# Threshold attention and a tanh-shrink MLP on one core: the shared tiles of two head pairs made one duo, turns and transfers re-timed

## The chip, the cores and the metric

One core of a Trainium2 chip runs the whole kernel. The metric is the device time of one execution in microseconds, and the median of several runs is compared. The profiler records one execution, and all views of the profile are of that one.

## The reference

Two layers follow each other. The first is attention with a threshold, for 8 batches, 8 heads, 576 rows and 64 columns:

```python
scores = scale * np.matmul(q, k.transpose(0, 1, 3, 2))
thresh = np.max(scores, axis=-1, keepdims=True) - tau
scores = np.where(scores >= thresh, scores, -1000000000.0)
scores = scores - np.max(scores, axis=-1, keepdims=True)
attn = np.exp(scores)
attn = attn / (np.sum(attn, axis=-1, keepdims=True) + 1e-09)
return np.matmul(attn, v).astype(np.float32)
```

The second takes the heads side by side as rows `x` of 512 (4608 rows), and computes `h = x @ w_in` (512 to 2048), `g = h - tanh(h)` and `g @ w_out` (2048 to 512). All inputs and the output are float32.

## The kernel before

**Pairs, tiles, duos.** The work goes by pairs of heads: 32 pairs, four to a batch (a batch is called a block below). A head has 576 rows, that is four tiles of 128 rows and a rest of 64. The rests of both heads of a pair fill one *shared* tile, so a pair has nine tiles (`TPP = 9`) and the kernel 288. Tile number `i` is tile `j = i % 9` of pair `p = i // 9`: 0 to 3 are head 0, 4 is the shared one, 5 to 8 are head 1. Two neighbouring tiles of one head form a *duo* ("A" and "B", `kind`), which shares one maximum buffer, one `nb`, one transpose and one `pT`. The shared tile ("M") goes alone: it has an `nb` of its own, buffers `zm` padded to 640 columns, and a transpose of five blocks where a duo has one of nine.

**A tile's way.** `scores` multiplies a tile of qT with kT and with kS (kT with its halves exchanged, which adds the low-order parts of the float16 split) into PSUM, and VectorE scales it into `sc` and takes its maximum (L337). `shift` makes `nb`, the threshold (L354). `kink` is a steep Prelu on ScalarE (L374), which gives `z`. For pairs 0 to 5 (`on_pe`) TensorE transposes z (L394). From pair 6 on the DMA crossbar does (`zT<-z`, L382, issued from SP). `weights` is the exponential on ScalarE (L403 or L411), which gives `pT`. `attend` multiplies pT with v (L440, for the shared tile L429) into `psO`; v has a column of ones that collects the sum. The five blocks of a tile's weights are four of 128 keys and one of 64; in a duo, the two blocks of 64 lie in one block, in rows 0 to 63 and 64 to 127, and v's buffer `vb` has two matching chunks (4 and 5), each zero in the other half. `norm` divides a head's output by its sum on VectorE (L454, L455, and L460 for the shared tile, at head 0). `emit_x` transposes a pair's output on TensorE (L472, L478) and copies it (L485, L486) into the MLP's input.

**Preparing a pair.** `load` brings k, q, v from SP. `split` (GpSimd, L190 to L194) makes the float16 parts khl and qhl. `turn` transposes them: nine matmuls on TensorE (L241) into the same two-buffer PSUM ring `big` that the scores use, then a copy on VectorE (L264). For k, GpSimd then makes kS with two copies (L270). From pair 8 on, q of the odd pairs and of pair 30 is turned by the crossbar instead (`q_by_dma`, L253). `split_v` (GpSimd, L222 to L227) fills vb.

**MLP.** Beside the attention of a block, the MLP of the block before it runs: `hidden` (L495), tanh on ScalarE (L508), `g` on VectorE (L514), `project` (L521), and every fourth step a copy `yo` (L534) and a store (L537), which is issued when the next one is ready. A step is four matmuls of 512 columns. `layers` deals about one step to a slot (fewer in the first block), and none to the first four slots of a block.

**Order.** No planner sets the order: the program is written out slot by slot, `s` from -8 to 292, and every engine takes its instructions in the order in which the slots issue them. In slot `s` come: `shift` of tile s+7, `scores` of tile s+8 (`AHEAD = 8`), `kink` of tile s+5, tanh, `weights` of tile s, an MLP step, g, stores, `attend` of tile s-2 (`LAG = 2`) with `norm` and `emit_x`, then the steps of `plan` for the slot, and casts of the MLP's weights on GpSimd (until about slot 59). (For the first four pairs weights and attend come four slots earlier.) `plan` puts the preparation of pair p a number `d` of slots before its first scores, in slot 9p - 8 - d: loads at d = 16, 15, 14 for k, q, v, splits of k and q at 8 and 7, turn k at 5, split_v at 4, turn q at 3, or at 5 by the crossbar.

**Buffers** that matter here: PSUM ring `big` two (scores and turns), `psO` one, `psH` two, `psY` one; pT three, zT six, z four, raw two of each of k, q, v, vb four.

Of the kernel before, what the change touches and what calls it, by code (L numbers as in the profile page):

```python
# [18 lines left out]
def kernel(  # L19
# [11 lines left out]
    nc = tc.nc  # L31
# [15 lines left out]
    NPAIR = B * HPAIR  # L47
    DM_C = d_model // P
    DF_C = d_ff // P
    TPP = 9  # L50
    NTILE = NPAIR * TPP

# [34 lines left out]
    for i in range(NV):  # L87
# [3 lines left out]
        nc.gpsimd.memset(vb[0:64, :, 4, D : D + 1], 1.0)  # L91
        nc.gpsimd.memset(vb[64:P, :, 5, D : D + 1], 1.0)
        vbs.append(vb)

    NM = 2
    zms = []
    for i in range(NM):
        zm = const.tile([P, 5 * P], BF16, name=f"zm{i}")
        nc.vector.memset(zm[:, S : 5 * P], -STEEP)
        zms.append(zm)  # L100

    mx3 = []
# [39 lines left out]
    def load(p, t):  # L144
        b, h0 = p // HPAIR, 2 * (p % HPAIR)
        hs = slice(h0, h0 + 2)
        src = {"k": k, "q": q, "v": v}[t]
        eng = nc.sync
        r = raws[p, t] = raw_pool.tile([P, 10, D], F32, name=f"{t}raw", tag=t)
        n = 8 if t == "v" else 10  # L150
        eng.dma_start(
            out=r[:, 0:n, :].rearrange("p (h c) d -> p h (c d)", h=2)[:, :, 0 : 4 * D],
            in_=src[b, hs, 0:512, :].rearrange("h (p c) d -> p h (c d)", c=4),
        )
        rem = src[b, hs, 512:S, :].rearrange("h s d -> s h d")
        if t == "v":
            eng.dma_start(out=r[0:64, 8:10, :], in_=rem)
        else:
            eng.dma_start(out=r[:, 4, :], in_=rem)
# [136 lines left out]
    REM = (slice(512, 576), slice(576, 640))  # L296
    scs, mxs, nbs, zs, zts, pts, ops = {}, {}, {}, {}, {}, {}, {}

    def kind(j):

        return "M" if j == 4 else "A" if j in (0, 2, 5, 7) else "B"

    def scores(i):
        p, j = divmod(i, TPP)
        qT, kT, kS = mats[p, "q"], mats[p, "k"], mats[p, "ks"]
        ps = ps_big.tile([P, 1024], F32, name="psS", tag="big")
        main, rem, lo = slice(0, 512), slice(512, 576), 0
        if kind(j) == "B":
            main, rem, lo = slice(512, 1024), slice(448, 512), 448
        if j == 4:  # L310
            qrem = REM
            if q_by_dma(p):
                qrem = (slice(512, 640, 2), slice(513, 640, 2))
            for n, kk in enumerate((kT, kS)):
                for dst, srcs in ((main, MAIN), (rem, REM)):
                    for hh in range(2):
                        nc.tensor.matmul(  # L317
                            out=ps[64 * hh : 64 * hh + 64, dst],
                            lhsT=qT[:, qrem[hh]], rhs=kk[:, srcs[hh]],
                            start=(n == 0), stop=(n == 1),  # L320
                        )
        else:
            hh = int(j > 4)
            lhs = qT[:, j * P : (j + 1) * P]
            for n, kk in enumerate((kT, kS)):
                for dst, src in ((main, MAIN[hh]), (rem, REM[hh])):
                    nc.tensor.matmul(  # L327
                        out=ps[:, dst], lhsT=lhs, rhs=kk[:, src],
                        start=(n == 0), stop=(n == 1),
                    )  # L330
        sc = sc_pool.tile([P, S], F32, name="sc")
        if kind(j) == "B":
            mx = mxs[i] = mxs.pop(i - 1)
        else:
            mx = mxs[i] = mx3[i // 2 % len(mx3)]
        c = int(kind(j) == "B")
        nc.vector.tensor_scalar(  # L337
            out=sc, in0=ps[:, lo : lo + S], scalar1=SC, scalar2=None,
            op0=ALU.mult, op1=ALU.max, accum_out=mx[:, c : c + 1],
        )  # L340
        scs[i] = sc

    def shift(i):

        kd = kind(i % TPP)
        if kd == "A":
            return
        mx = mxs.pop(i)
        nb = st_pool.tile([P, 9], F32, name="nb", tag="nb")
        o, m = nb[:, 0:1], mx[:, 0:1]  # L350
        if kd == "B":
            o = nb.rearrange("p (a b) -> p a b", b=3)[:, :, 0:2]
            m = mx.rearrange("p (a b) -> p a b", b=4)[:, :, 0:3]
        nc.vector.tensor_scalar(  # L354
            out=o, in0=m, scalar1=-1.0, scalar2=tau, op0=ALU.mult, op1=ALU.add
        )
        if kd == "B":
            nbs[i - 1], nbs[i] = nb[:, 0:1], nb[:, 1:2]
        else:
            nbs[i] = nb[:, 0:1]  # L360

    def kink(i):
        sc, nb = scs.pop(i), nbs.pop(i)
        kd = kind(i % TPP)
        if kd == "B":
            zt = zs.pop(i - 1)
            z = zt[:, S:W]
        elif kd == "A":
            zt = zs[i] = z_pool.tile([P, W], BF16, name="z")
            z = zt[:, 0:S]  # L370
        else:
            zt = zms[i // TPP % NM]
            z = zt[:, 0:S]
        nc.scalar.activation(  # L374
            out=z, in_=sc, func=ACT.Prelu, bias=nb, scale=1.0, alpha=STEEP
        )
        if on_pe(i):
            zts[i] = zt
        elif kd != "A":
            n = 5 if kd == "M" else TPP  # L380
            zts[i] = zt_pool.tile([P, TPP, P], BF16, name="zT")
            nc.sync.dma_start_transpose(out=zts[i][:, 0:n, :], in_=zt)  # L382

    def weights(i):


        kd = kind(i % TPP)
        n, off = {"A": (4, 0), "M": (5, 0), "B": (5, 4)}[kd]
        if on_pe(i):
            z = zts.pop(i)  # L390
            pl, tag = (ps_h, "h") if i % 2 and i < HPAIR * TPP else (ps_y, "y")
# [23 lines left out]

    def attend(i):

        p, j = divmod(i, TPP)
        kd, vb = kind(j), vbs[p % NV]
        if kd == "A":  # L420
            return
        if j in (1, 6):
            ops[p, int(j > 4)] = ps_o.tile([P, 6, D + 1], F32, name="psO", tag="o")
        po = ops[p, int(j > 4)]
        if kd == "M":
            pt = pts.pop(i)

            for c in range(5):
                nc.tensor.matmul(  # L429
                    out=po[:, 4:6, :], lhsT=pt[:, c * P : (c + 1) * P],  # L430
                    rhs=vb[:, :, c, :], start=(c == 0), stop=(c == 4),
                )
            return
        pt, hh = pts.pop(i), int(j > 4)

        for ab in range(2):
            blocks = [(4 * ab + ab + c, c) for c in range(4)]
            blocks.append((4, 4 + ab))
            for n, (blk, c) in enumerate(blocks):
                nc.tensor.matmul(  # L440
                    out=po[:, (j - 1 - 5 * hh) + ab, :],
                    lhsT=pt[:, blk * P : (blk + 1) * P], rhs=vb[:, hh, c, :],
                    start=(n == 0), stop=(n == 4),
                )

    osb = {}

    def norm(p, hh):
        po = ops.pop((p, hh))
        if hh == 0:  # L450
            osb[p] = o_pool.tile([P, 5, 2, D], BF16, name="osb")
        n = 5 - hh
        rc = st_pool.tile([P, 5], F32, name="rc", tag="rc")
        nc.vector.reciprocal(out=rc[:, 0:n], in_=po[:, 0:n, D])  # L454
        nc.vector.tensor_tensor(  # L455
            out=osb[p][:, 0:4, hh, :], in0=po[:, 0:4, 0:D],
            in1=rc[:, 0:4].unsqueeze(2).to_broadcast([P, 4, D]), op=ALU.mult,
        )
        if hh == 0:
            nc.vector.scalar_tensor_tensor(  # L460
                out=osb[p][:, 4, :, :], in0=po[:, 4:6, 0:D], scalar=rc[:, 4:5],
                in1=own, op0=ALU.mult, op1=ALU.mult,
            )
# [55 lines left out]
    def project(m, ms, part, ps, last, cols=slice(0, d_model)):  # L519
# [5 lines left out]
        if part == 3:  # L525
# [8 lines left out]
                nc.vector.tensor_copy(out=yo, in_=ps)  # L534
            if m < B:
                rows = out[m * S : m * S + MB, :].rearrange("(p c) n -> c p n", c=4)
                stores.append(lambda: nc.sync.dma_start(out=rows[ms], in_=yo))  # L537
            else:
                for h in range(2):
                    b = 2 * ms + h  # L540
                    eng = nc.scalar if h and nc_ < d_model else nc.sync
                    stores.append(
                        lambda b=b, h=h, eng=eng: eng.dma_start(
                            out=out[b * S + MB : (b + 1) * S, cols],
                            in_=yo[64 * h : 64 * h + 64, :],
                        )
                    )
# [107 lines left out]
    for p in range(1, NPAIR):  # L655
        first = TPP * p - AHEAD
        for d, f in PREP[3 if p == 1 else 0 :]:
            d -= p == 1 and d in (3, 5)
            plan.setdefault(first - d, []).append(lambda p=p, f=f: f(p))
        d = 5 if q_by_dma(p) else 3 - (p == 1)  # L660
        plan.setdefault(first - d, []).append(lambda p=p: turn(p, "q"))

    load(0, "v")
# [27 lines left out]
    for s in range(-AHEAD, NTILE + LAG + 3):  # L691
# [37 lines left out]
        for i in atts.pop(s, []):  # L729
            pp, jj = divmod(i, TPP)  # L730
            if i < NTILE:
                attend(i)
            if i < NTILE and jj in (4, 8):
                norm(pp, int(jj > 4))
            if jj == 1 and pp:
                emit_x(pp - 1)
        for step in plan.pop(s, []):
            step()
# [61 lines left out]
```

## Time and profile before

| | before |
|---|---|
| median of 8 runs | 536.83 us (536.49 to 538.35) |
| the profiled execution | 537.43 us, of which the span of the profile is 535.6 |
| TensorE busy | 513.5 us, 96% |
| VectorE busy | 427.4 us, 80% |
| ScalarE busy | 438.0 us, 82% |
| GpSimd busy | 290.0 us, 54% |
| transposes of z, z with padding, q by the crossbar | 104, 26, 13 |
| loads of v; stores of 256 KB | 32 and 32 (a large and a small one); 32 |
| DMA traffic | 85.76 MB, 160 GB/s in the mean |

The busy times are shares of the whole span, which has stages with different limits, so the table alone does not say which engine sets the time. The time that TensorE's instructions are shown for is modelled at its end and overlaps with the next instruction; how far the starts of two matmuls lie apart is the better measure. "PEld" is the load of a matmul's stationary side. A wait for several signals is put down to the one that came last.

### The profile page before, as it was taken

How to read it: one execution, taken by the hardware profiler on the slowest of the kernel's cores; microseconds unless marked ns; L12 is line 12 of the kernel's file. 1: busy time of each engine (PE TensorE's matmuls, PEld its weight loads, DVE VectorE, ACT ScalarE, POOL GpSimd, SP SyncE). 2: the span in 40 equal slices, each digit the busy share in tenths (PEclk: the TensorE clock that was granted, in tenths of full speed). 3: DMA queues.
4: the chain of work that ended last, by engine and by line, in shares of the span. 5: the costliest groups of instructions: out<-in, count | busy, mean ns of one | idle time of the engine just before them, and what ended most of it. 6: DMA issues, size and time to landing. Idle time of an engine off the chain costs nothing.

```text
span 535.6 us, 13042 instructions
## 1 busy us (share of the span) xinstructions
PE 513.5 (96%) x4782; PEld 288.5 (54%) x4782; DVE 427.4 (80%) x1202; ACT 438.0 (82%) x630; POOL 290.0 (54%) x390
## 2 busy tenths in 40 slices
PE   8989899999999999999999999999999999999997
PEld 4666565555555555555555555555455455444444
DVE  5889878989888988889888988898888888554440
ACT  5999888998898989899888989898989989543330
POOL 7999995767555666666555755565665720000000
PEclk9999999999999999999999999999999999999999
DMA  7554657999899799799999999899988975401113
GB/s 211 174 185 146 207 163 139 198 189 184 174 177 184 178 188 196 168 181 188 187 187 185 192 192 187 157 182 197 189 157 184 188 153 111 105 21 39 39 41 78
DMA packets 204768, 85.76 MB, mean 160 GB/s; under 512 B 172320, under 2 KB 197152, under 8 KB 204704
## 3 DMA queue, kind: packets, MB, share of 16 engines
q1 hardware_dynamic: 204112, 84.51, 74.9%
q8 instruction: 37, 0.61, 0.5%
q10 hardware_dynamic: 592, 0.43, 0.3%
q14 instruction: 27, 0.22, 0.1%
HBM read 36.70 MB, written 9.44 MB: 86 GB/s over the span
## 4 chain that ended last, share of the span: by engine, by line
PE 67%; DVE 14%; POOL 8%; DMA 3%; issue 3%; ACT 2%; SPq 1%; DVEq 0%; POOLq 0%; ACTq 0%
PE psY L521 21%; PE psH L495 17%; PE psS L327 14%; DVE sc L337 6%; PE psO L440 5%; DVE g L514 3%; PE psS L317 3%; PE psHt L495 3%; POOL kS L270 2%; PE ps_k L241 2%; DMA qT<-qhl 2%; DVE kT L264 1%; DVE yo L534 1%; POOL w_in_sb L628 1%; POOL khl L194 1%
## 5 line engine op out<-in xcount | busy, mean ns | idle before, releaser
L337 DVE TENSOR_SCALAR_CACHE_REDUCE sc<-psS 128x576 f32<-128x576 f32 x288 | 216.1, 752 | 23.2 <-PE psS L327 14.7
L374 ACT ACTIVATE z<-sc,nb 128x576 bf16<-128x576 f32 x256 | 193.5, 768 | 19.0 <-DVE nb L354 18.9
L521 PE MATMUL psY<-w_out_sb,g 128*128 128x512 bf16 (+1 forms) x592 | 146.0, 374 | 0.8 <-DVE yo L534 0.8
L411 ACT ACTIVATE pT<-zT 128x1152 f16<-128x1152 bf16 (+1 forms) x130 | 138.9, 1068 | 1.6 <-PE psS L327 1.0
L270 POOL COPY kS<-kT 64x1152 f16<-64x1152 f16 x62 | 70.7, 1141 | 127.5 <-DVE nb L354 125.8
L495 PE MATMUL psH<-xT,w_in_sb 128*128 128x512 bf16 x480 | 124.0, 379 | 2.3 <-DVE g L514 2.3
L327 PE MATMUL psS<-kT,qT 128*128 128x512 f16 (+1 forms) x512 | 104.4, 285 | 7.2 <-DVE sc L337 4.2
L508 ACT ACTIVATE th<-psH 128x512 f32<-128x512 f32 x128 | 75.4, 589 | 36.9 <-PE psH L495 35.7
L327 PEld LDWEIGHTS <-qT 128*128 128x128 f16 x1024 | 72.5, 97 | 57.1 <-issue 9.2
L327 PE MATMUL psS<-kS,qT 128*128 128x512 f16 x496 | 101.4, 286 | 0.8 <-POOL kS L270 0.7
L514 DVE SCALAR_TENSOR_TENSOR g<-th,psH 128x512 bf16<-128x512 f32 x128 | 87.3, 682 | 17.9 <-ACT th L508 17.9
L521 PEld LDWEIGHTS <-g 128*128 128x128 bf16 x592 | 50.7, 98 | 56.8 <-issue 4.0
L495 PEld LDWEIGHTS <-w_in_sb 128*128 128x128 bf16 x576 | 49.2, 98 | 58.2 <-issue 4.5
L440 PEld LDWEIGHTS <-pT 128*128 128x128 f16 x1280 | 55.7, 98 | 25.2 <-issue 1.9
L440 PE MATMUL psO<-vb,pT 128*128 128x65 bf16 x1280 | 61.2, 193 | 0.0
L194 POOL TENSOR_TENSOR khl<-kraw,khl 128x576 f16<-128x576 f32 x31 | 39.7, 1279 | 2.6
L194 POOL TENSOR_TENSOR qhl<-qraw,qhl 128x576 f16<-128x576 f32 x31 | 39.7, 1279 | 2.7
L403 ACT ACTIVATE pT<-psZ 128x640 f16<-128x640 bf16 (+1 forms) x54 | 35.4, 658 | 5.8 <-PE psZ L394 5.4
L264 DVE COPY kT<-ps_k 128x1152 f16<-128x1152 f16 x31 | 23.4, 756 | 14.0 <-PE ps_k L241 14.0
L534 DVE COPY yo<-psY 128x512 f32<-128x512 f32 (+1 forms) x31 | 21.1, 682 | 13.1 <-PE psY L521 11.1
L455 DVE TENSOR_TENSOR osb<-psO,rc 128x256 bf16<-128x256 f32 x64 | 27.2, 424 | 2.2
L354 DVE TENSOR_SCALAR nb<-mx 128x6 f32<-128x6 f32 (+1 forms) x160 | 24.5, 153 | 2.3
(81 smaller groups left out, 509.3 us busy)
## 6 DMA issues: line engine op xcount, KB each, us to landing
vraw<-in_v_dram SPq DMA_DIRECT2D x32, 256.0 KB, 3.5
out_dram<-yo SPq DMA_DIRECT2D x32, 256.0 KB, 3.0
kraw<-in_k_dram SPq DMA_DIRECT2D x31, 256.0 KB, 3.3
qraw<-in_q_dram SPq DMA_DIRECT2D x31, 256.0 KB, 3.7
wt<-in_moe_w_in_dram SPq DMA_DIRECT2D x8, 512.0 KB, 4.3
wt<-in_moe_w_out_dram SPq DMA_DIRECT2D x8, 512.0 KB, 4.4
zT<-z SPq DMA_TRANSPOSE x104, 3.5
kraw<-in_k_dram SPq DMA_DIRECT2D x32, 32.0 KB, 3.0
```

What stands on the lines that cost most here:

```text
L194: nc.gpsimd.tensor_tensor(out=hl[:, :, 1, :], in0=x, in1=hl[:, :, 0, :], op=ALU.subtract)
L270: nc.gpsimd.tensor_copy(out=o, in_=i)
L327: nc.tensor.matmul(out=ps[:, dst], lhsT=lhs, rhs=kk[:, src], start=(n == 0), stop=(n == 1),)
L337: nc.vector.tensor_scalar(out=sc, in0=ps[:, lo : lo + S], scalar1=SC, scalar2=None, op0=ALU.mult, op1=ALU.max, accum_out=mx[:, c : c + 1],)
L374: nc.scalar.activation(out=z, in_=sc, func=ACT.Prelu, bias=nb, scale=1.0, alpha=STEEP)
L403: nc.scalar.activation(out=pt[:, off * P : (off + n) * P], in_=ps[:, 0 : n * P], func=ACT.Exp)
L411: nc.scalar.activation(out=pt[:, 0 : n * P], in_=zts.pop(i)[:, 0:n, :], func=ACT.Exp)
L440: nc.tensor.matmul(out=po[:, (j - 1 - 5 * hh) + ab, :], lhsT=pt[:, blk * P : (blk + 1) * P], rhs=vb[:, hh, c, :], start=(n == 0), stop=(n ...
L495: nc.tensor.matmul(out=ps, lhsT=w_in_sb[:, c, n * P : (n + 1) * P], rhs=xs[m][:, c, :] if m < B else xR[:, c, :, :], start=(c == 0), stop= ...
L508: nc.scalar.activation(out=th, in_=ps, func=ACT.Tanh)
L514: nc.vector.scalar_tensor_tensor(out=gs[m][:, n, :], in0=th, scalar=-1.0, in1=ps, op0=ALU.mult, op1=ALU.add,)
L521: nc.tensor.matmul(out=ps, lhsT=gs[m][:, n, ms * P : (ms + 1) * P], rhs=w_out_sb[:, n, cols], start=(n == 0), stop=(n == DF_C - 1),)
```

## The change

- **Shared duo.** The shared tile moves to the end of an even pair and to the beginning of an odd one, so that the shared tiles of two pairs are neighbours and form a duo like any other. `kind` is now the parity of i, and `place` gives the pair, head and tile of i. The kind "M" and the buffers `zm` go. The transposes become one of nine blocks for every two tiles.
- **Attend.** A duo's block of 64 + 64 keys is multiplied once with both chunks of v (130 columns, for both tiles), then eight matmuls of 65 columns add to that. The shared duo's two halves are done by `attend_shared` when psO of the head with which they share a buffer is there: head 1 of the even pair, head 0 of the odd one. `skip_group_check` is a flag of the builder.
- **Norms.** They follow the tiles: jj = 3 (even pair) or 4 (odd) for head 0, jj = 0 of the next pair (even) or 8 (odd) for head 1. `emit_x` of an even pair comes one slot later.
- **Turns.** Turn k is at d = 6 (odd) or 3 (even) from pair 5 on. Turn q on TensorE is at d = 2, only for pair 3 still at 3.
- **q by the crossbar.** Its turn is at d = 7, and the splits of k and q of these pairs are at 10 and 9.
- **Queues.** The loads of v from pair 8 on, and the stores of blocks 0 to 5, are issued from GpSimd's queue in place of SP's.

```diff
-    def kind(j):
-        return "M" if j == 4 else "A" if j in (0, 2, 5, 7) else "B"
+    def kind(i):
+        return "AB"[i % 2]
+    def place(i):
+        p, j = divmod(i, TPP)
+        j = j - p % 2
+        return (p, None, 4) if j in (-1, 8) else (p, j // 4, j % 4)
...
-        eng = nc.sync
+        eng = nc.gpsimd if t == "v" and p >= 2 * HPAIR else nc.sync
...
     def kink(i):
...
-            n = 5 if kd == "M" else TPP
             zts[i] = zt_pool.tile([P, TPP, P], BF16, name="zT")
-            nc.sync.dma_start_transpose(out=zts[i][:, 0:n, :], in_=zt)
+            nc.sync.dma_start_transpose(out=zts[i], in_=zt)
...
     def attend(i):
...
-        for ab in range(2):
-            blocks = [(4 * ab + ab + c, c) for c in range(4)]
-            blocks.append((4, 4 + ab))
-            for n, (blk, c) in enumerate(blocks):
-                nc.tensor.matmul(
-                    out=po[:, (j - 1 - 5 * hh) + ab, :],
-                    lhsT=pt[:, blk * P : (blk + 1) * P], rhs=vb[:, hh, c, :],
-                    start=(n == 0), stop=(n == 4),
-                )
+        p, hh, t = place(i)
+        vb, pt = vbs[p % NV], pts[i]
+        if hh is None:
+            attend_shared(p - 1, 0, pt)
             return
+        if t == 1:
+            ops[p, hh] = ps_o.tile([P, 6, D + 1], F32, name="psO", tag="o")
+            if p % 2 and hh == 0:
+                attend_shared(p, 1, pts.pop(i - 2))
+        po = ops[p, hh]
+        nc.tensor.matmul(
+            out=po[:, t - 1 : t + 1, :], lhsT=pt[:, 4 * P : 5 * P],
+            rhs=vb[:, hh, 4:6, :], start=True, stop=False, skip_group_check=True,
+        )
+        for n in range(8):
+            ab, c = divmod(n, 4)
+            blk = 5 * ab + c
+            nc.tensor.matmul(
+                out=po[:, t - 1 + ab, :], lhsT=pt[:, blk * P : (blk + 1) * P],
+                rhs=vb[:, hh, c, :], start=False, stop=(n == 7), skip_group_check=True,
+            )
+    def attend_shared(p, ab, pt):
+        vb = vbs[p % NV]
+        for n in range(5):
+            blk, c = ((5 * ab + n, n) if n < 4 else (4, 4 + ab))
+            nc.tensor.matmul(
+                out=ops[p, 1 - p % 2][:, 4:6, :], lhsT=pt[:, blk * P : (blk + 1) * P],
+                rhs=vb[:, :, c, :], start=(n == 0), stop=(n == 4),
+            )
...
-                stores.append(lambda: nc.sync.dma_start(out=rows[ms], in_=yo))
+                eng = nc.gpsimd if m < B - 2 else nc.sync
+                stores.append(lambda: eng.dma_start(out=rows[ms], in_=yo))
...
             d -= p == 1 and d in (3, 5)
+            if d in (7, 8) and q_by_dma(p):
+                d = d + 2
+            if d == 5 and p >= 5:
+                d = 6 if p % 2 else 3
...
-        d = 5 if q_by_dma(p) else 3 - (p == 1)
+        d = 7 if q_by_dma(p) else 3 - (p == 1 or p % 2 == 0 or p >= 5)
...
-            if i < NTILE and jj in (4, 8):
-                norm(pp, int(jj > 4))
-            if jj == 1 and pp:
+                odd = pp % 2
+                if jj == 3 + odd:
+                    norm(pp, 0)
+                elif odd and jj in (0, 8):
+                    norm(pp - (jj == 0), 1)
+            if pp and jj == 1 + pp % 2:
                 emit_x(pp - 1)
```

## The prediction

> **What bounds the kernel now.** I read the page's first part, then the time windows by stage, the list of waits, and the timeline where the windows left a question. From the page (a group's columns: line, engine, operation, tiles, count | busy us, mean ns of one | idle before it):
>
> ```profile
> PE 513.5 (96%) x4782; PEld 288.5 (54%) x4782; DVE 427.4 (80%) x1202; ACT 438.0 (82%) x630; POOL 290.0 (54%) x390
> L440 PE MATMUL psO<-vb,pT 128*128 128x65 bf16 x1280 | 61.2, 193 | 0.0
> L270 POOL COPY kS<-kT 64x1152 f16<-64x1152 f16 x62 | 70.7, 1141 | 127.5 <-DVE nb L354 125.8
> ```
>
> The windows (stretch, its length, busy us and instructions of PE, PEld, DVE, ACT, POOL; then clock, DMA share, GB/s) show that 96% is a mean of stages:
>
> ```profile
> 26.00:37.00 11.00, 10.33 (x149) 7.50 (x149) 10.00 (x31) 10.62 (x19) 10.41 (x14) 1.00 0.52 169
> 100.00:115.00 15.00, 13.87 (x154) 8.21 (x150) 13.96 (x40) 14.86 (x22) 10.87 (x13) 1.00 0.98 178
> 250.00:350.00 100.00, 99.00 (x932) 54.97 (x930) 87.54 (x250) 89.49 (x124) 57.14 (x73) 1.00 0.95 182
> ```
>
> Until about 72 us ScalarE (10.62 of 11.00) and GpSimd (10.41) are full, and TensorE has gaps. Around 100 us ScalarE is full. From about 130 us to the end TensorE is: 99.00 of 100. There only fewer TensorE instructions or fewer TensorE waits shorten the kernel. Its waits from 100 to 440 us:
>
> ```profile
> POOL kS L270 <- DVE nb L354: 121.9, 24, 6.6
> DVE kT L264 <- PE ps_k L241: 10.9, 17, 1.1
> PE psS L327 <- DVE sc L337: 2.2, 11, 0.3
> PEld L327 <- DMA qT<-qhl: 2.6, 3, 1.4
> PE psS L327 <- DMA qT<-qhl: 1.4, 2, 1.0
> ```
>
> The two last lines partly tell of the same moments (weight load and matmul both stand still), so the crossbar's q costs TensorE about 1.4 us, not 4.0. GpSimd's 121.9 us are idle time before kS, which waits for the copy kT.
>
> [...] ten of 65 columns take 257.98 to 258.29 us, 31 ns each; five of 130 take 260.15 to 260.44, 58 ns each (below). [...] No run before issues a load from GpSimd. [...]
>
> **Part 1, attend.** Before, each of 128 duos takes ten matmuls of 65 columns; after, one of 130 and eight of 65. The columns are 650 both times. A pair of 65s costs 62 ns, a 130 costs 58: 4 ns a duo, 128 x 4 = 0.5 us[...]. The 193 ns mean of the group row is latency and must not be used, nor 61.2/1280 = 48 ns. **I take -0.6 (0 to -0.9).** The shared part keeps its 160 matmuls of 130 columns, the shared scores all of theirs.
>
> **Part 2, ten transposes become nine.** In pairs 6 to 31, 26 exponentials of 640 columns at 726 ns (18.9 us) become 13 of 1152 at 1154 (15.0): ScalarE saves 3.9 us, 0.15 a pair. VectorE's nb go from 160 to 144 of 155 ns, 24.5 us to 22.3. SP loses 13 transposes of about 1.3 us issue time. In steady state all this lies beside TensorE's 99% and is worth nothing. In pairs 6 to 8, where ScalarE is full, 3 x 0.15. **-0.4 (0 to -1).** A shared pT lives two slots longer in the ring of three: its next writer comes at slot i+6, its last reader at i+4, so two slots (3.2 us) stay: nothing.
>
> **Part 3, the turns of k and q.** Count slots modulo 18 from the first of an even pair. Norms: before 6, 10, 15, 1; after 5, 11, 15, 1. Turn k: before 5 and 14; after (pair 5 on) 7 and 13. Turn q on TensorE: before 7, after 8. Before, q followed a norm at once; at 89 us this cost 0.82 us:
>
> ```profile
> 89.28 0.67 PE L241 MATMUL ps_q<-ident_f,qhl 128*128 128x128 f16 x9
> 89.36 0.42 DVE L455 TENSOR_TENSOR osb<-psO,rc 128x256 bf16<-128x256 f32 x1
> ...
> 90.77 0.41 PE L327 MATMUL psS<-kT,qT 128*128 128x512 f16 x2 [0.82 <-DVE sc L337]
> ```
>
> The norm (0.19+0.42+0.34 us) held back sc, and the turn had taken the other buffer of the ring of two. All waits of TensorE for sc are 4.2 us on the full list of waits; about 0.25 us in each block stands where the MLP pauses, and stays. **-1.5 (0 to -3)** with the smaller waits from 86 to 131 us. Against it stands **kS**. An even pair's k is now turned three slots ahead of its scores instead of five. The chain in the trace:
>
> ```profile
> 257.98 0.48 PE L440 MATMUL psO<-vb,pT 128*128 128x65 bf16 x10
> 258.29 0.67 PE L241 MATMUL ps_k<-ident_f,khl 128*128 128x128 f16 x9
> ...
> 259.06 0.76 DVE L264 COPY kT<-ps_k 128x1152 f16<-128x1152 f16 x1 [0.44 <-PE ps_k L241]
> ...
> 259.95 2.32 POOL L270 COPY kS<-kT 64x1152 f16<-64x1152 f16 x2 [5.86 <-DVE nb L354]
> ...
> 260.15 0.46 PE L429 MATMUL psO<-vb,pT 128*128 128x130 bf16 x5
> ...
> 260.44 0.41 PE L327 MATMUL psS<-kT,qT 128*128 128x512 f16 x2
> ```
>
> kS ends 262.27 - 258.29 = 3.98 us after the turn starts. TensorE's work until it reads kS: the turn 0.51, slot 8 (scores 0.49, an MLP step 0.86, turn q 0.51) 1.86, slot 9 (0.49 + 0.86 + attend 0.31) 1.66, the kT half of the scores 0.24: 4.27. The margin is 0.29 us, and a norm two slots earlier (0.95 us) may leave VectorE late. GpSimd itself is free by then: split_v is in slot 6, its next split waits in slot 9. **+0.7 (0 to +6.5)**, over 13 even pairs, 0.05 each. Odd pairs have six slots; that their turn k now shares slot 13 with emit_x (0.42 + 0.21 us of VectorE) costs nothing there.
>
> **Part 4, q for the crossbar two slots sooner.** Splits and turn move together, so their distance stays; load to split shrinks from eight slots to six (9.6 us, against 3.3 to land). SP comes late today because transposes wait for ScalarE ahead of q in one queue:
>
> ```profile
> 421.51 1.31 SPq L253 DMA_TRANSPOSE qT<-qhl  x1
> ...
> 425.10 0.42 PE L327 MATMUL psS<-kT,qT 128*128 128x512 f16 x2 [0.95 <-DMA qT<-qhl]
> ```
>
> Two slots (3.2 us) cover 0.95. But the splits for it now follow kS of slot 7 at once: kS until about slot 9.5, two splits of 2.6 us, qhl about slot 12.8, so SP, due at 12, waits about a slot; the z transposes behind it have about two. **-1.4 (0 to -1.6).**
>
> **Part 5, v loads and stores from GpSimd.** 24 pairs x 2 loads and 6 blocks x 4 stores, 72 issues, leave SP (0.54 to 0.65 us each, 42 us) for GpSimd. No row shows one[...]. A store waits for yo, but is issued a step of y (8 slots) later, so splits and kS behind it don't wait; v loads come ten slots ahead of split_v, raw buffers long free. The cover is GpSimd's idle time before kS. **0 (-0.5 to +3).**
>
> **Sum:** -0.6 - 0.4 - 1.5 + 0.7 - 1.4 = -3.2 us on the profiled execution, 537.43 (span 535.6 and 1.8 around it): 534.2. That execution lies 0.6 over the median of 536.83, so I forecast 533.6. Little is to be had beyond: TensorE's own waits from 100 to 440 us add to 6.3 us in that list, and the first 72 us are GpSimd's, where only turn q of pairs 2 and 4 moves, by a slot.
>
> **Rivals.** *A, as above* (0.67): 530.5 to 535.6. *B, a wait for a wait* (0.13): q comes in time, but TensorE stands as long at kS or sc; gains of 3.9 are eaten: 536 to 537.5. For it: VectorE at 88% and ScalarE at 89% have little give. Against: kT waited for TensorE, not TensorE for it. *C, kS late* (0.13): in even pairs kT gets behind one sc and one g (0.75 + 0.68 us). Each such stall is 1.43 - 0.29 = 1.1 us, in all 13 pairs 14.8, and 548 at the end. It decides from 0.3 us a pair (3.9/13), when kT starts 0.6 us later after its turn than now; at 0.5 us it gives 6.5 - 3.9 = +2.6: 539.4. For it: the norm in slot 5. Against: VectorE stood idle 0.44 us before kT. *D, GpSimd as bound* (0.04): three issues fill its 6.2 us a pair from 2.1 us each[...]. *E* (0.03): the crossbar engines are full at 0.95 whoever issues, and SP gains nothing; about 535.0, the sum without part 4.
>
> **Numbers.** Faster 0.69 (A and most of E), same 0.14 (B, the rest of E), slower 0.17 (C, D); 0.2%, 1.1 us, is about what a measurement can tell. The range takes A's lower bounds together at 529.5 and C's nearer half at 540.
>
> **Right if** the waits show no DMA qT, PE waits for kS stay under 1 us in all, windows from 150 us show TensorE at 99% with about 0.1 us less per block of four pairs, and GpSimd's idle time before kS falls to 50 us or more. **Wrong if** kS heads TensorE's waits, or GpSimd's idle time is gone and khl or qhl are waited for.

## The result, and the profile after

| | before | after |
|---|---|---|
| median | 537.25 us (32 runs, 536.41 to 538.57) | 571.5 us (11 runs, 562.89 to 577.2) |
| profiled execution (span) | 537.43 us (535.6) | 569.36 us (567.6) |
| ratio after to before | | 1.0544 [1.0523, 1.0566] |

The change makes the kernel slower by 5.4%, where 533.6 us were forecast. (The ratio leaves out runs over 1.5% above the fastest of a kernel, so it stands for some 566.5 us, and a difference that this text takes from the median of all eleven, 571.5, would be 5.0 us smaller with it.)

First the page of the kernel after: busy times, the granted clock in 40 slices, the two large DMA queues (packets, MB, share of 16 engines' span), and groups (line, engine, operation, tiles, count | busy us, mean ns of one | idle before it and what ended most of it).

```profile
PE 521.8 (92%) x4651; PEld 293.9 (52%) x4651; DVE 424.4 (75%) x1184; ACT 437.1 (77%) x617; POOL 334.8 (59%) x462
...
PEclk9999999988989799897998999999999899999999
...
q1 hardware_dynamic: 188592, 70.71, 63.5%
q0 software_dynamic: 4608, 13.37, 9.4%
...
L400 ACT ACTIVATE pT<-zT 128x1152 f16<-128x1152 bf16 x117 | 135.0, 1154 | 32.7 <-DMA zT<-z 32.6
L265 POOL COPY kS<-kT 64x1152 f16<-64x1152 f16 x62 | 70.7, 1141 | 117.7 <-DVE nb L349 116.1
L428 PE MATMUL psO<-vb,pT 128*128 128x65 bf16 x1024 | 54.4, 196 | 0.0
L421 PE MATMUL psO<-vb,pT 128*128 128x130 bf16 x128 | 28.5, 223 | 25.4 <-ACT pT L400 25.4
```

TensorE's share fell from 96% to 92% with 131 instructions fewer. GpSimd's busy time grew by 44.8 us, which are the new issues, and its idle time before kS only fell from 125.8 to 116.1 us: GpSimd is not what is short. New are two idle times: ScalarE's exponential waits 32.6 us for zT, a crossbar transpose, and TensorE's attend waits 25.4 us for that exponential. The granted clock has slices at 7 and 8, early and in the middle. Queue q0 is GpSimd's own: 13.37 MB in 4608 packets, 2.9 KB each in the mean.

The windows of the same stretches as before, and one short one (stretch, length, busy us and instructions of PE, PEld, DVE, ACT, POOL; clock, DMA share, GB/s):

```profile
26.00:37.00 11.00, 9.75 (x139) 7.16 (x137) 10.15 (x31) 10.39 (x18) 10.41 (x14) 1.00 0.52 171
100.00:115.00 15.00, 14.16 (x143) 8.47 (x140) 14.71 (x41) 14.48 (x21) 9.98 (x14) 1.00 0.86 157
250.00:350.00 100.00, 92.69 (x823) 51.46 (x821) 81.05 (x232) 82.65 (x112) 66.40 (x89) 0.95 0.89 169
350.00:470.00 120.00, 115.81 (x1056) 64.78 (x1054) 102.27 (x290) 105.34 (x143) 83.97 (x114) 0.99 0.91 177
124.00:130.00 6.00, 3.80 (x23) 2.13 (x24) 1.39 (x5) 4.88 (x6) 3.65 (x6) 0.56 0.80 184
```

Up to 115 us nothing is lost. From 250 to 350 us TensorE starts 823 matmuls where it started 932 before (911 in `e1_all_on_sp` below, which has the same instructions), and no other engine is full. From 124 to 130 us the granted clock is 0.56. Counted in the trace, ScalarE has six long waits for zT: they begin between 120 and 292 us, 34 to 35 us apart, one in every two pairs (18 slots), and make up 28.7 of its 32.6 us. A block takes 67 to 68 us there, and about 58 afterwards, as in the kernel before.

The waits of the kernel after from 100 to 470 us (engine, line, what it waited for: us in all, times, longest):

```profile
ACT pT L400 <- DMA zT<-z: 32.6, 10, 6.0
...
PE psO L421 <- ACT pT L400: 25.4, 9, 5.3
```

No wait of TensorE for qT is left, and none for kS over 0.3 us. One of the stalls in its timeline (start us, duration, engine, line, operation; in brackets the idle time before it and what ended it):

```profile
149.01 1.15 ACT L400 ACTIVATE pT<-zT 128x1152 f16<-128x1152 bf16 x1
...
149.69 14.40 SPq L371 DMA_TRANSPOSE zT<-z  x4
...
150.10 0.72 POOL L146 DMA_DIRECT2D vraw<-in_v_dram  x1
...
150.81 0.60 POOL L152 DMA_DIRECT2D vraw<-in_v_dram  x1
...
151.99 1.15 ACT L400 ACTIVATE pT<-zT 128x1152 f16<-128x1152 bf16 x1
...
155.45 0.62 POOL L537 DMA_DIRECT2D out_dram<-yo  x1
...
157.79 1.03 PE L520 MATMUL psY<-w_out_sb,g 128*128 128x512 bf16 x4
...
160.94 1.16 ACT L400 ACTIVATE pT<-zT 128x1152 f16<-128x1152 bf16 x1 [5.98 <-DMA zT<-z]
...
162.15 0.27 PE L421 MATMUL psO<-vb,pT 128*128 128x130 bf16 x1 [3.34 <-ACT pT L400]
```

The exponentials stand at 149.01, 151.99 and then 160.94: for the last, ScalarE stood idle 5.98 us. Before that, a v load leaves GpSimd at 150.10, 0.41 us after SP began to issue transposes of z at 149.69. SP's first three issues from there on take 1.67, 2.51 and 6.38 us where the median is 1.38: SP is held up in issuing. The store of 155.45 falls into the same stretch. Its windows:

```profile
146.00:152.00 6.00, 6.00 (x53) 3.28 (x51) 5.83 (x17) 4.89 (x9) 4.08 (x5) 1.00 1.03 214
152.00:158.00 6.00, 6.00 (x57) 2.98 (x56) 4.32 (x15) 2.95 (x5) 5.51 (x10) 1.00 1.18 86
158.00:162.00 4.00, 0.82 (x4) 0.20 (x2) 1.45 (x3) 1.06 (x1) 3.33 (x6) 1.00 1.29 140
```

The last two columns are to be read together: from 152 to 158 us the DMA engines show as full as ever (1.18), yet only 86 GB/s pass, against 214 just before. (The share adds up the times of all packets, which overlap, so it can exceed 1.) Counted in the trace, the packets of the v load's 288 KB took from 151.9 to 158.5 us, 6.5 us, where 1 to 4 are usual outside the six stalls. Those of 4 KB took 0.65 us each in the mean, where 0.17 is the median of all. Of the 256-byte packets of the transposes most still took 18 ns, but some took up to 1 us, so that their mean from 152 to 158 us was 69 ns, against 26 over the stretch from 100 to 480 us. The view of the tile zT in the kernel after sums it up: duration of an issue, minimum/median/maximum, and from issue to landing:

```profile
L371 SPq DMA_TRANSPOSE zT<-z x117: 1272/1377/6376, 85.4 to 490.1; - x117
...
DMA to landing us min/median/max: 3.2/3.5/11.6
```

In the kernel before, the last line was:

```profile
DMA to landing us min/median/max: 2.5/3.4/6.8
```

The median hardly moved, the tail is new.

### The profile page after: what moved, and what is told of

Read it like the earlier page. It is cut to its first block, busy times and chain, and to the rows that moved or that the text cites. A ratio compares the mean times of both kernels' runs of the same rounds, so it can differ in the third digit from the quotient of the medians.

```text
span 567.6 us, 12777 instructions
## 1 busy us (share of the span) xinstructions
PE 521.8 (92%) x4651; PEld 293.9 (52%) x4651; DVE 424.4 (75%) x1184; ACT 437.1 (77%) x617; POOL 334.8 (59%) x462
## 3 DMA queue, kind: packets, MB, share of 16 engines
q0 software_dynamic: 4608, 13.37, 9.4%
## 4 chain that ended last, share of the span: by engine, by line
PE 60%; POOL 10%; DMA 10%; DVE 7%; ACT 7%; issue 5%; SPq 0%; ACTq 0%; POOLq 0%; DVEq 0%
PE psY L520 18%; PE psH L494 16%; PE psS L327 13%; DMA zT<-z 9%; PE psO L428 3%; ACT z L364 3%; PE psHt L494 2%; POOL kS L265 2%; DVE sc L337 2%; DVE g L513 2%; PE ps_k L236 2%; ACT pT L400 2%; POOL khl L189 1%; ACT th L507 1%; PE psS L318 1%
## 5 line engine op out<-in xcount | busy, mean ns | idle before, releaser
L364 ACT ACTIVATE z<-sc,nb 128x576 bf16<-128x576 f32 x288 | 216.6, 769 | 33.6 <-DVE nb L349 31.6
L400 ACT ACTIVATE pT<-zT 128x1152 f16<-128x1152 bf16 x117 | 135.0, 1154 | 32.7 <-DMA zT<-z 32.6
L265 POOL COPY kS<-kT 64x1152 f16<-64x1152 f16 x62 | 70.7, 1141 | 117.7 <-DVE nb L349 116.1
L494 PE MATMUL psH<-xT,w_in_sb 128*128 128x512 bf16 x480 | 128.6, 392 | 3.5 <-DVE g L513 3.5
L327 PE MATMUL psS<-kT,qT 128*128 128x512 f16 (+1 forms) x512 | 107.0, 291 | 4.0 <-DVE sc L337 2.1
L327 PEld LDWEIGHTS <-qT 128*128 128x128 f16 x1024 | 75.9, 99 | 62.0 <-issue 10.9
L327 PE MATMUL psS<-kS,qT 128*128 128x512 f16 x496 | 103.8, 292 | 0.0
L494 PEld LDWEIGHTS <-w_in_sb 128*128 128x128 bf16 x576 | 50.3, 100 | 61.3 <-issue 11.4
L428 PE MATMUL psO<-vb,pT 128*128 128x65 bf16 x1024 | 54.4, 196 | 0.0
L421 PE MATMUL psO<-vb,pT 128*128 128x130 bf16 x128 | 28.5, 223 | 25.4 <-ACT pT L400 25.4
L428 PEld LDWEIGHTS <-pT 128*128 128x128 f16 x1024 | 45.2, 99 | 9.3
L392 ACT ACTIVATE pT<-psZ 128x512 f16<-128x512 bf16 (+1 forms) x54 | 35.0, 652 | 5.4 <-PE psZ L383 5.2
L421 PEld LDWEIGHTS <-pT 128*128 128x128 f16 x128 | 12.5, 98 | 39.8 <-ACT pT L400 28.7
L533 DVE COPY yo<-psY 128x512 f32<-128x512 f32 (+1 forms) x31 | 21.1, 682 | 14.4 <-PE psY L520 12.7
```

The costliest lines, as they stand in the source:

```text
L265: nc.gpsimd.tensor_copy(out=o, in_=i)
L327: nc.tensor.matmul(out=ps[:, dst], lhsT=lhs, rhs=kk[:, src], start=(n == 0), stop=(n == 1),)
L364: nc.scalar.activation(out=z, in_=sc, func=ACT.Prelu, bias=nb, scale=1.0, alpha=STEEP)
L400: nc.scalar.activation(out=pt[:, 0 : n * P], in_=zts.pop(i)[:, 0:n, :], func=ACT.Exp)
L421: nc.tensor.matmul(out=po[:, t - 1 : t + 1, :], lhsT=pt[:, 4 * P : 5 * P], rhs=vb[:, hh, 4:6, :], start=True, stop=False, skip_group_check ...
L428: nc.tensor.matmul(out=po[:, t - 1 + ab, :], lhsT=pt[:, blk * P : (blk + 1) * P], rhs=vb[:, hh, c, :], start=False, stop=(n == 7), skip_gr ...
```

## The experiments

Theory 1, formed from these lines: the transfers issued from GpSimd hold up the crossbar's transposes in the DMA engines, zT is late, TensorE stands, and its granted clock falls. The rivals: the new order or the sooner q alone makes zT late, whoever issues the loads; a collision of a certain slot, which a shift of the load would remove; or the bytes, not the queue. All times are medians; "ratio" is to the kernel before, run beside it.

**All loads and stores back on SP** (`e1_all_on_sp`), the rest of the change kept:

```diff
-        eng = nc.gpsimd if t == "v" and p >= 2 * HPAIR else nc.sync
+        eng = nc.sync
...
-                eng = nc.gpsimd if m < B - 2 else nc.sync
+                eng = nc.sync
```

> The kernel after, with v loads and stores back on SP's queue; all else of the change stays. Theory 1 (two queues at once: transfers from GpSimd's queue run in the DMA engines between the packets of the crossbar's transposes, zT lands late, ScalarE waits for zT and TensorE for pT): the waits of ScalarE for zT fall from 32.6 us to under 2 us, the granted clock is 1.00 again, and the time is 531 to 537 us. Theory 2 (the new order itself makes the transposes late, since q's transpose and the splits stand in front of them): the waits for zT stay above 20 us and the time stays above 560 us. Theory 3 (kS late on even pairs): TensorE waits for kS for several us and the time is 538 to 548 us.

533.49 us, ratio 0.9925 [0.9905, 0.9946]. This one part is worth 38.0 us (33.0 with the 566.5 us of the ratio) and the sign; the kernel without it beats both. Its page, window and tile zT:

```profile
PE 510.6 (96%) x4651; PEld 289.5 (54%) x4651; DVE 423.9 (80%) x1184; ACT 436.3 (82%) x617; POOL 290.4 (55%) x390
```

```profile
250.00:350.00 100.00, 99.12 (x911) 55.95 (x911) 88.29 (x251) 89.53 (x121) 60.36 (x78) 1.00 0.91 183
```

```profile
L371 SPq DMA_TRANSPOSE zT<-z x117: 1242/1344/2953, 85.4 to 454.1; - x117
...
DMA to landing us min/median/max: 3.2/3.6/6.8
```

TensorE is back at 99.12 of 100 us, and no zT lands later than 6.8 us. The waits from 100 to 440 us, ScalarE's and then TensorE's:

```profile
ACT pT L400 <- DMA zT<-z: 4.5, 6, 1.5
```

```profile
PE psO L421 <- ACT pT L400: 0.7, 1, 0.7
...
PE psS L327 <- POOL kS L265: 0.3, 1, 0.3
```

The spans differ by 567.6 - 531.4 = 36.2 us. TensorE's wait for pT grew by 24.7. The matmuls at half clock, counted in the trace of the kernel after (seven stretches; matmuls of 512 columns start up to 427 ns apart in place of 216), lose some 12 us: 9.0 by 46 matmuls of 512 columns, and 2.6 by smaller ones. Together that is about the whole difference; two such counts can't tell a last microsecond.

**One of the two transfers each** (`e2_v_on_pool`: stores on SP; `e3_stores_on_pool`: v on SP), each one half of the diff above.

> The kernel after, with only the stores back on SP; v loads from pair 8 on stay on GpSimd's queue. Theory 1, with v loads as the disturbing transfer (295 KB a pair in packets of up to 4 KB): 558 to 572 us, with 20 us or more of ScalarE waiting for zT. If the stores are what disturbs: 531 to 540 us. Theory 2: above 560 us as well, so this run alone doesn't tell 1 from 2.

> The kernel after, with only the v loads back on SP; stores of blocks 0 to 5 stay on GpSimd's queue. Theory 1 with v loads as the disturbing transfer: 531 to 540 us, waits for zT of at most 5 us[...]. If the stores disturb as much as loads, byte for byte (6.3 MB of 13.4 MB): 545 to 555 us. Theory 2: above 560 us.

v alone: 545.62 us, 1.0138 [1.0097, 1.0179]. Stores alone: 535.0, 0.9964 [0.9943, 0.9985]. So v costs 12.1, the stores 1.5, and both together 38.0: they don't add. For v alone I had expected 558 to 572 us and 20 us or more of waiting for zT. The waits with v alone, from 100 us on:

```profile
ACT pT L400 <- DMA zT<-z: 14.4, 7, 4.5
...
PE psO L421 <- ACT pT L400: 11.0, 4, 4.8
```

TensorE's 11.0 us are of the same wait, and near the 12.1.

**The queues alone in the kernel before** (`e4_before_pool`), by the same two lines the other way round, **and with q sooner** (`e8_before_pool_q`):

```diff
+            if d in (7, 8) and q_by_dma(p):
+                d = d + 2
...
-        d = 5 if q_by_dma(p) else 3 - (p == 1)
+        d = 7 if q_by_dma(p) else 3 - (p == 1)
```

> The kernel before, with nothing of the change but its queues: v loads from pair 8 on and stores of blocks 0 to 5 issued from GpSimd. Theory 1: slower than before by 10 to 35 us (548 to 572 us), with ScalarE waiting for zT for 10 us or more. Theory 2, and theory 3: within 2 us of before, 535 to 539 us. If the queues disturb only together with the new places of q's transposes, a value between.

> The kernel before with v loads and stores on GpSimd's queue (540.8 us) and, beyond that, the crossbar's q two slots sooner with its splits. If q's place is the trigger: 555 us or more. If the order of tiles is (nine evenly spaced transposes and turns at 7 and 13): 537 to 543 us, rather less than 540.8, since the wait for q goes.

540.79 us, 1.0062 [1.0044, 1.0081], and 544.71, 1.0127 [1.0094, 1.0161]. My numbers for the first were far off: in the old order the queues cost 3.5 us, not tens. A wait is there, but TensorE waits for qT (first line) and ScalarE for zT only 0.7. With q sooner the wait moves to zT (second line), yet queues and q together cost only some 7 us here:

```profile
PE psS L327 <- DMA qT<-qhl: 3.6, 3, 2.0
```

```profile
ACT pT L411 <- DMA zT<-z: 10.2, 4, 3.6
```

**q back in the kernel after** (`e7_q_back`), and **q back with all on SP** (`e12_q_old`):

```diff
-                d = d + 2
+                d = d + 0
...
-        d = 7 if q_by_dma(p) else 3 - (p == 1 or p % 2 == 0 or p >= 5)
+        d = 5 if q_by_dma(p) else 3 - (p == 1 or p % 2 == 0 or p >= 5)
```

> The kernel after, queues and all, but the crossbar's q and its splits are back at the old distances (d = 5, splits at 8 and 7). SP's queue then has q's transpose in slot 14 after the k and q loads. Theory 1c, if q's transpose ahead of the loads is what makes the z transposes pile up: below 550 us. Theory 1d: 560 to 575 us, as after. Theory 2 (q's place alone) is already answered by 533.5 us with all on SP.

> All on SP, with the crossbar's q and its splits back at the old distances (5; 8 and 7). By part 4 of the prediction this loses 1.4 us (534.9) and TensorE waits for q again. If q sooner is a burden to z's transposes even on one queue, it is faster than 533.5, since 4.5 us of waiting for zT go.

546.37 us, 1.0176 [1.0126, 1.0227], and 534.97, 0.9954 [0.9942, 0.9966]. The waits with q back and the new queues:

```profile
PE psS L318 <- DMA qT<-qhl: 12.3, 7, 2.9
ACT pT L400 <- DMA zT<-z: 1.9, 1, 1.9
```

So the new queues cost 3.5 us in the old order, 11.4 in the new one with q at its old place (546.37 - 534.97), and 38.0 in the new one with q sooner. The transfers hold up transposes of either kind: q, for which TensorE waits by itself, or z, behind which come ScalarE, then TensorE; the clock follows in both (0.992 granted in the mean in `e7_q_back`, 0.970 in the kernel after). With the queues q sooner costs 25.1 us in the new order, some 4 in the old one (544.71 - 540.79); without them it brings 1.5. So the 38.0 us need three things at once, the queues, q sooner and the new order of tiles and turns. What in that order matters, no run tried.

**v loaded four slots later** (`e6_v_four_later`), for a collision with one certain transpose:

```diff
+            d -= 4 * (d == LDK - 2 and p >= 2 * HPAIR)
```

> The kernel after, queues and all, but the v loads from pair 8 on are issued four slots later (d = 10 instead of 14: slots 0 and 9 of the eighteen instead of 14 and 5). Theory 1c (it is a collision in time: SP has q's transpose and four loads of k and q in slots 12 and 13, so z transposes pile up just when the v load comes in slot 14): below 545 us, with few waits for zT. Theory 1d (the two queues disturb each other wherever they meet): 560 us or more.

574.17 us, 1.0642 [1.057, 1.0713], and ScalarE waits for zT as before:

```profile
ACT pT L400 <- DMA zT<-z: 32.1, 10, 4.8
```

It is not the one slot in which the v load stood: SP issues a transpose every two slots, so that a v load finds one to hold up in the other place too. That rival falls, as far as two places tell. The place of q's transpose on SP does matter: in `e7_q_back` my expectation gave a time below 550 us to pile-up behind that transpose, and 546.37 came.

**v from ScalarE's queue** (`e5_v_on_act`), stores on SP, and **the stores from ScalarE's queue** with v on GpSimd (`e16_stores_on_act`):

```diff
-        eng = nc.gpsimd if t == "v" and p >= 2 * HPAIR else nc.sync
+        eng = nc.scalar if t == "v" and p >= 2 * HPAIR else nc.sync
```

```diff
-                eng = nc.gpsimd if m < B - 2 else nc.sync
+                eng = nc.scalar if m < B - 2 else nc.sync
```

> The kernel after with stores on SP and v loads from pair 8 on issued from ScalarE's queue: a second queue beside the transposes, as with GpSimd, but a hardware one, whose packets for the same loads should be 1 KB as on SP and not 4 KB. Compare with v loads on GpSimd alone (545.6) and all on SP (533.5). Theory 1a (any second queue disturbs the transposes): 541 to 550 us and ScalarE waits for zT for 10 us or more. Theory 1b (GpSimd's descriptors are what disturbs): 532 to 537 us, the issue on ScalarE costing it about 48 short instructions that the trace hardly shows.

> The kernel after, v loads on GpSimd's queue, but the stores of blocks 0 to 5 on ScalarE's. If it is the stores' leaving SP that brings v loads alone (545.6) to 571.5: 560 to 575 us. If it is that stores and v loads stand in one and the same software queue: 543 to 552 us.

538.1 us, 1.0012 [0.9997, 1.0027], and 549.43, 1.0217 [1.0182, 1.0252]. With v on ScalarE's queue TensorE waits for pT:

```profile
PE psO L421 <- ACT pT L400: 4.1, 5, 1.9
```

Against all on SP v costs 4.6 us from ScalarE's queue, which the profile lists as a hardware queue like SP's, and 12.1 from GpSimd's: it lies between the two theories. Not all of the 4.6 need be a second queue beside the transposes. ScalarE issues in the order of its other work, and the 48 issues take some 25 us of it; its wait for zT grows only from 4.5 to 5.2 us, and about 1 of TensorE's 4.1 us falls where zT was in time and ScalarE was behind after such an issue (at 405.4 us). The run doesn't part the two. v on GpSimd and stores on ScalarE's queue cost 3.8 more than v alone, where stores on GpSimd as well cost 25.9: most of what didn't add goes when the stores leave GpSimd's queue (and perhaps with their packets, which are of 4 KB there and of 2 KB from SP's queue in the kernel before).

**A spare v load that nobody reads**, beside the real one, with all else on SP: 256 KB, from GpSimd (`e14_spare_pool`) or from SP (`e15_spare_sp`). This adds traffic and leaves the computation as it is.

```diff
+        if t == "v" and p >= 2 * HPAIR:
+            nc.gpsimd.dma_start(
+                out=spare.rearrange("p (h c) d -> p h (c d)", h=2),
+                in_=src[b, hs, 0:512, :].rearrange("h (p c) d -> p h (c d)", c=4),
+            )
```

> All on SP, and beyond that each v load of 256 KB from pair 8 on is done a second time into a spare buffer that nobody reads, from GpSimd's queue. Nothing waits for it; it only takes room in the DMA engines and 0.7 us of GpSimd's idle time. Theory 1 (a transfer from a second queue, amid the transposes, holds them up): 540 to 560 us with ScalarE waiting for zT for 10 us or more. If only lateness of GpSimd's or SP's own work counts: within 2 us of 533.5.

> The same spare load, from SP's queue: the same bytes in the same place of the order, but in line with the transposes. Theory 1: below the run with the spare load on GpSimd by 8 us or more, 534 to 540 us. If it is the bytes that count and not the queue: the same time as that run within 2 us.

546.15 us, 1.0166 [1.0093, 1.0239], and 538.54, 1.0028 [1.0015, 1.0041]. TensorE's wait for the exponential, first from GpSimd, then from SP:

```profile
PE psO L427 <- ACT pT L406: 11.3, 8, 4.5
```

```profile
PE psO L427 <- ACT pT L406: 1.9, 4, 1.3
```

The same bytes cost 5.0 us over `e1_all_on_sp` from SP and 12.7 from GpSimd. Nobody reads these bytes, so that the cost isn't a late v; and 7.6 of the 12.7 come with the other queue, whose packets were larger for the v loads (mostly 4 KB in the kernel after, against 1 KB from SP). (The four runs from GpSimd lie between 542.94 and 549.84 us, so that the 7.6 is good to some 4 us.)

**The kink one slot sooner**, so that z has a slot more, in the kernel after (`e9_z_slot_sooner`) and with all on SP (`e13_sp_z_sooner`):

```diff
-    MASK = 5
+    MASK = 6
```

> The kernel after, queues and all, with kink one slot sooner (MASK = 6, so z is made six slots ahead of its exponential in place of five): nothing in the DMA engines changes but each z transpose has one slot, 1.6 us, more time. Theory 4 (the loss is the little slack of z: transposes that come late by more than it stop ScalarE, TensorE and then the clock): well below 571.5, 540 to 558 us, with ScalarE waiting for zT for less than 15 us. Theory 5 (the DMA engines lose throughput with two queues and the backlog grows until something waits): within 5 us of 571.5.

> All on SP, with kink one slot sooner (MASK = 6): the control for the 554.9 us of the same step with GpSimd's queues. Theory 4 (with a slot more, the queues cost nothing; what is left is the price of the earlier kink itself, ScalarE waiting for nb): within 3 us of 554.9. Theory 5 (part of the queues' loss stays in the engines): 535 to 548 us, and the difference to 554.9 is that part.

554.89 us, 1.0324 [1.031, 1.0337], and 554.58, 1.0318 [1.03, 1.0337]. The waits for zT are gone and the clock is 1.0, and the queues cost 0.3 us. But the sooner kink has a price of its own, 21.1 us with all on SP, since it catches up with the shift; the line is the same in both kernels, here that of the second:

```profile
ACT z L364 <- DVE nb L349: 43.7, 69, 1.8
```

The lost time does go by way of zT's slack, then. A kernel with 21 us more also has more room everywhere, so that this run doesn't show alone that one slot would do.

**The old turns** (`e10_turns_old`) and **the old attend** (`e11_attend_old`), both with all on SP:

```diff
-            if d == 5 and p >= 5:
-                d = 6 if p % 2 else 3
...
-        d = 7 if q_by_dma(p) else 3 - (p == 1 or p % 2 == 0 or p >= 5)
+        d = 7 if q_by_dma(p) else 3 - (p == 1)
```

```diff
-        nc.tensor.matmul(
-            out=po[:, t - 1 : t + 1, :], lhsT=pt[:, 4 * P : 5 * P],
-            rhs=vb[:, hh, 4:6, :], start=True, stop=False, skip_group_check=True,
-        )
...
+        for ab in range(2):
+            blocks = [(5 * ab + c, c) for c in range(4)]
+            blocks.append((4, 4 + ab))
```

> All on SP (533.5 us), with the turns of k and of TensorE's q back at the old distances (5 and 3). By part 3 of the prediction (-1.5 with +0.7 against it) this loses 0.8 us, 534.3, and brings back waits of TensorE for sc behind a turn next to a norm. If kS were late in the new places by more than 0.7 us, it is faster than 533.5.

> All on SP, with ten matmuls of 65 columns for a duo again in place of one of 130 and eight of 65; tiles, norms and turns as after. By part 1 of the prediction this loses 0.6 us (534.1). [...]

539.2 us, 1.0035 [1.0023, 1.0047], and 535.12, 0.9964 [0.995, 0.9978]: 5.7 and 1.6 us over `e1_all_on_sp`. With the old turns TensorE's scores wait for kT:

```profile
PE psS L327 <- DVE kT L259: 4.5, 7, 1.4
```

## Why the prediction was wrong

**The step that failed is part 5**, "0 (-0.5 to +3)"; it measured +38.0 us (571.5 against 533.49). It priced the 72 issues as GpSimd's time alone. No run before had shown such an issue, and their time is not what was short: 44.8 us for 72 is 0.62 us each, the longest took 0.93 us. "The cover is GpSimd's idle time before kS" held as well, with 116.1 us of it left. What it never asked is what these transfers meet in the DMA engines: that another issuer changes no more than who spends the issue time was assumed, and no run had shown it. The runs show what a second queue costs here when its neighbour is a crossbar transpose: zT landed up to 11.6 us after its issue, ScalarE waited 32.6 us for it and TensorE 25.4 us for ScalarE, and with the loads and stores back on SP these waits fell to 4.5 and 0.7 us.

One difference between the queues is the size of their packets: GpSimd's v loads mostly go in packets of 4 KB, the same loads from SP's or ScalarE's queue in 1 KB, and v costs 12.1 us against 4.6 from ScalarE's. That larger packets hold up the transposes longer fits this in direction, but how the engines share their time between two queues was not shown. The amount doesn't fit. A v load from GpSimd has 64 packets of 4 KB and 16 of 2 KB, four and one for each of 16 engines if they are dealt evenly; at their usual 0.17 and 0.08 us, letting all of them pass would delay a transpose by some 0.8 us (an estimate from these counts), where the three of the stall above landed 7 to 8 us later than the median. There packets of both queues became slow themselves, and why is open. Packet size alone wasn't tried: from SP to ScalarE the queue changes and the size stays, from there to GpSimd both change.

**Part 4's slack is the second half of the failure.** "The z transposes behind it have about two" slots, 3.2 us, beyond a landing of 3.4 to 3.5: true of the median, and useless against a tail of 11.6 us. I weighed q's delay ahead of z (SP waited for qhl only 2.9 us in all, 12 times, less than the slot that I gave it each time), not a delay of the transposes themselves.

**The half clock was in no step.** In the kernel after TensorE has six waits of 2.5 to 5.3 us for pT, and during each of them, or within 0.6 us of its end, begins a stretch of 3.4 or 6.8 us in which the trace shows half the clock granted; a seventh such stretch, at 298.7 us, came with waits of 0.9 and 1.3 us. From 124 to 130 us the mean is 0.56, and matmuls start 427 ns apart in place of 216. It made 25.4 us of standing into some 37.

**The other parts stood in sum.** All of them without part 5 were forecast at 533.6 us and measured 533.49. That it meets so closely is in part luck: taken out one at a time, attend, turns and q measured 1.6, 5.7 and 1.5 us, where 0.6, 0.8 and 1.4 were forecast, and these alone add up to 8.8, more than twice the 3.8 us that the kernel without part 5 gains in all. The parts aren't independent:
- Part 1 (-0.6): taking it out costs 1.6. The mechanism is confirmed: counted over all 128 duos, the next instruction of TensorE starts 312.5 ns after the attend's first matmul in `e1_all_on_sp` (median) and 317.0 ns in the kernel before and in `e11_attend_old`. That is 4.5 ns a duo and 0.6 us in all, as forecast. For the other 1.0 us a zT late by 1.8 us in the profile of `e11_attend_old` is a likely reason, not a shown one. A duo in `e1_all_on_sp`:

```profile
254.65 0.22 PE L421 MATMUL psO<-vb,pT 128*128 128x130 bf16 x1
...
254.70 0.42 PE L428 MATMUL psO<-vb,pT 128*128 128x65 bf16 x8
...
254.96 0.38 PE L471 MATMUL psX<-ident_bf,osb 128*128 128x128 bf16 x4
```

- Part 2 (-0.4) has no run of its own. VectorE's busy time fell from 427.4 to 423.9 us, ScalarE's from 438.0 to 436.3, and whether that bought any time beside a full TensorE no run shows.
- Part 3 (-1.5, and +0.7 for kS): the margin of 0.29 us held, with one wait for kS of 0.3 us. The 5.7 us of the old turns, for which I expected 0.8, are no measure of the -1.5, because they stand in the new order of norms; they say that the new order needs the new turns.
- Part 4 (-1.4 for qT's wait): 1.5 measured, and with q at its old place TensorE waits for qT again, 3.0 and 0.9 us, of which the time shows less than half:

```profile
PE psS L318 <- DMA qT<-qhl: 3.0, 4, 1.3
...
PE psS L327 <- DMA qT<-qhl: 0.9, 1, 0.9
```

**The rivals.** B and C fell: neither kS nor sc took over. (A's lower bounds add up to 529.8 us, not 529.5, which changes nothing.) D, the only one with a bad end for part 5, had the right part and the wrong resource: GpSimd's time instead of the DMA engines'. (Its 6.2 us a pair are what 57.14 us busy in 100 leave of the 14.44 us from pair to pair, the crossbar's q standing at 116.6 and 434.2 us for pairs 9 and 31.) E named the engines, "full at 0.95 whoever issues", and drew from it that the issuer doesn't matter. The issuer, with the packets that come with it, is just what mattered. The sign "GpSimd's idle time before kS falls to 50 us or more" came out right in a kernel slower by 5%: it tested the cover, not the cost.

**Open:** why loads and stores in GpSimd's queue cost so much more together than apart (38.0 against 13.6; the first stall comes before GpSimd's first store, at 144.8 us), and why the long stalls end at about 310 us although loads and stores go on. One rival is untested: in each of the six stalls, between the issue and the landing of the late transposes, the DMA engines also bring a 16 KB block of instructions (queue q8), at 157.1 us in the one shown. Shortly after it, from 159 to 160 us, only 4 GB/s passed. Gaps of about 1 us follow many of these fetches in the kernel before as well (from 100 to 440 us, 14 of 25 have within 3 us a microsecond in which under 15 GB/s started, where 19% of all stretches of 3 us have one), and a fetch beside a v load at 320.4 us brought no long stall, so fetches alone are not the cause; they may lengthen a stall.

## What to carry to other kernels

Before moving a transfer to another issuer, ask what is in flight on the DMA engines beside it, and who waits for that; if it is a transpose with two slots of slack, keep the bulk transfers in the transposes' own queue, which was the cheapest place here (v from SP 533.49 us, from ScalarE 538.1, from GpSimd 545.62). Judge the slack of a transfer by the tail of its landing times, not by the median, and count a stall of TensorE with the half clock that comes with it: here 25.4 us of standing made some 37. And when a change bundles several edits, run the bundle without its riskiest one: here five edits brought 3.8 us and the sixth took 38.

## What the hardware showed that was not expected

- The same v load of 256 KB goes in packets of mostly 4 KB from GpSimd's queue, and of 1 KB from SP's or ScalarE's (with the stores, which go in 4 KB in place of 2 KB, 4608 packets for 13.37 MB, against some 13,400 more on q1 in `e1_all_on_sp`).
- Beside such a transfer a transpose of nine blocks landed up to 11.6 us after its issue in place of 6.8, and SP stood up to 6.4 us in one issue in place of 3.0.
- A spare load that nobody reads, 24 times 256 KB, costs 12.7 us from GpSimd and 5.0 from SP.
- DMA share is no measure of progress: 1.18 at 86 GB/s, 1.03 at 214, in neighbouring stretches of 6 us.
